# Thirty-two bytes further each time: the start addresses of the weight units and of the parts of g in a fused scan and two-layer kernel

## The chip, the core and the metric

The kernel runs on one core of one Trainium2 chip. The metric is the device time of one execution in microseconds (us). An execution was also recorded by the hardware profiler, and all rows shown here come from that one record.

## What is computed

The reference runs a gated state-space scan over 4 sequences of 768 positions with 8 heads, and sends its result through two dense layers with `h - tanh(h)` between them:

```python
# per head, in chunks along the sequence; cum = running sum of log a
M = (Cc @ Bc.T) * exp(cum_i - cum_j) * causal
y = M @ xc + (Cc @ state) * exp(cum_i)
state = exp(cum_last) * state + sum_j Bc_j x_j exp(cum_last - cum_j)
...
x = y laid out as (3072 tokens, 256)
h = x @ w_in                 # w_in  256 x 2048
g = h - tanh(h)
out = g @ w_out              # w_out 2048 x 256
```

Inputs are float32, but the two weight matrices arrive as 64-bit floats that the kernel converts on the chip.

## The kernel before

**Layers.** The tokens are cut into 12 tiles of 256 (`t`), the 2048 hidden columns into 8 units of 256 (`u`). A step is one pair (t, u). Its first part, `mm1` (line 545), makes 12 matmuls into the PSUM tile `ph`; its second, `mm2` (line 595), makes 12 into the PSUM tile `o`, where the units of a tile are summed. So there are 96 steps and 2304 matmuls of the two lines, and each is a weight load of 128 columns followed by a matmul that streams 256 columns.

**Why 12.** Each float32 operand is split into a high part, rounded to the matmul's float32r format, and the low rest: `xh`, `xl` for the input, `wh`, `wl` for the weights, `gh`, `gl` for g. A product is high by high, high by low and low by high. The stationary operand is always a 128-column piece of `wh` or `wl`; the moving operand is a 256-column piece of `xh`, `xl` (line 545) or of `gh`, `gl` (line 595).

**Around a step.** `act` takes `ph` to g: ACT's tanh (L559), DVE's subtraction (L563), ACT's rounding into `gh` (L567), DVE's rest into `gl` (L574). `g`, `gh` and `gl` each have three buffers of 128 x 512 elements in the pool `p3`. `mm2` of a step is emitted two steps after its `mm1`. Weights of a unit come once, by two DMAs, and `conv` makes `wh` (ACT, L318) and `wl` (DVE, L321) of them; both stay for the whole kernel:

```python
wh = cp.tile([P, NCONV, 2, 2, 256], F32R, name="wh")     # L284
wl = cp.tile([P, NCONV, 2, 2, 256], F32R, name="wl")     # L285
```

A unit is 2 x 2 x 256 elements, 4096 bytes in each partition.

**The scan** runs ahead of the tiles that need it, between steps. `chunk_a` makes the matmuls into `att` (lines 452 and 458: stationary operands of 9 and 16 rows), `chunk_y` those into `y` (line 494, stationary operands of 32 columns, and line 502, of 16 columns; the last chunk of a sequence has no line 502).

**Order.** The class `Order` records every operation with a cost and its dependencies, plans an order with list scheduling and random changes under a fixed seed, and emits the instructions in that order. It knows operations and named pieces of data, no addresses.

**Addresses before.** The allocator places tiles one behind another in each partition. Every unit of `wh` and `wl` starts at the same remainder after division by 512 bytes, and so do all buffers of `xh`, `xl`, `gh` and `gl`, at another; a table stands with the change.

Of the kernel before, what the change touches and what calls it, by code (L numbers as in the profile page):

```python
# [10 lines left out]
F32 = mybir.dt.float32  # L11
F32R = mybir.dt.float32r
# [4 lines left out]
ALU = mybir.AluOpType  # L17
# [3 lines left out]
P = 128  # L21
# [9 lines left out]
TT = 256  # L31
# [3 lines left out]
NCONV = NF // 2  # L35
# [6 lines left out]


NPH, NL, NSW, NRAW, NGB, LAG, WARM = 2, 3, 4, 2, 3, 2, 8
SWEEPS = 0, 2, 4, 6, 8


class Order:
# [12 lines left out]
    def slot(self, tag, bufs):  # L61
        k = self.count[tag] = self.count.get(tag, -1) + 1
        self.fresh[f"{tag}#{k}"] = tag, f"{tag}#{k - bufs}"
        return f"{tag}#{k}"
# [143 lines left out]
def tile_ssm_moe(ctx: ExitStack, tc: tile.TileContext, a, x, bn, bc, wts, out):  # L208
    nc = tc.nc
    cp = ctx.enter_context(tc.tile_pool(name="cp", bufs=1))  # L210
    p1 = ctx.enter_context(tc.tile_pool(name="p1", bufs=1))
    p2 = ctx.enter_context(tc.tile_pool(name="p2", bufs=2))
    p3 = ctx.enter_context(tc.tile_pool(name="p3", bufs=3))
# [6 lines left out]
    op = Order()  # L220
# [3 lines left out]
    raws, gs, po, n_po, obs, misc = {}, {}, {}, {}, {}, {}  # L224

    chunks, ends = {}, 0
    for t in range(NT):
        b, j = divmod(t, S // TT)
        end = b * CPB + -(-(j + 1) * TT // Q)
        chunks[t], ends = list(range(ends, end)), end  # L230
    wv, wm, pts, n_pt = {}, {}, {}, {}
    seq = {b: {} for b in range(NB)}
    KB = P * 1024

    SPAN = slice(len(chunks[0]), len(chunks[0]) + 7), slice(len(chunks[0]) + 7, NCK)


# [43 lines left out]
            op("SP", 0.42, lambda i=i: fn(i), w=[name[i]], dma=4 * KB)  # L281


    wh = cp.tile([P, NCONV, 2, 2, 256], F32R, name="wh")  # L284
    wl = cp.tile([P, NCONV, 2, 2, 256], F32R, name="wl")  # L285

    def conv(u, halves=False):
        raw, n = raws[u, 0], 2 if halves else 1
        n_v, n_m = op.pieces(slot("wv", 2), n), op.pieces(slot("wm", 1), n)

        def part(s, v):
            return v[:, s].bitcast(F32)

        def fn0(s):
            if s.start == 0:
                wv[u] = p2.tile([P, 2, 512], U32, tag="wv", name=f"wv{u}")
            nc.scalar.activation(part(s, wv[u]), raws[u][:, s, :, 1].bitcast(F32), AF.Copy, scale=REBIAS)

        def fn1(s):
            if s.start == 0:  # L300
                wm[u] = p1.tile([P, 2, 512], U32, tag="wm", name=f"wm{u}")
            nc.vector.tensor_scalar(out=wm[u][:, s], in0=raws[u][:, s, :, 0], scalar1=29, scalar2=None,
                                    op0=ALU.logical_shift_right)

        def fn2(s):
            vf = part(s, wv[u])
            nc.vector.tensor_scalar(out=vf, in0=vf, scalar1=-CLAMP, scalar2=CLAMP, op0=ALU.max, op1=ALU.min)

        def fn3(s):
            nc.vector.scalar_tensor_tensor(out=wm[u][:, s], in0=wv[u][:, s], scalar=3, in1=wm[u][:, s],  # L310
                                           op0=ALU.logical_shift_left, op1=ALU.bitwise_or)

        def fn4(s):
            nc.vector.scalar_tensor_tensor(out=wv[u][:, s], in0=wv[u][:, s], scalar=0x80000000, in1=wm[u][:, s],
                                           op0=ALU.bitwise_and, op1=ALU.bitwise_or)

        def hi(s):
            nc.scalar.copy(wh[:, u, s], part(s, wv[u]).rearrange("p i (k c) -> p i k c", k=2))  # L318

        def lo(s):  # L320
            nc.vector.tensor_tensor(out=wl[:, u, s], in0=part(s, wv[u]).rearrange("p i (k c) -> p i k c", k=2),  # L321
                                    in1=wh[:, u, s].bitcast(F32), op=ALU.subtract)

        for i in range(n):
            s, k = (slice(i, i + 1), 0.6) if halves else (slice(0, 2), 1.0)
            n_r = raw[s]
            n_h, n_l = [f"wh{u}.{j}" for j in range(2)][s], [f"wl{u}.{j}" for j in range(2)][s]
            op("ACT", 1.0 * k, lambda s=s: fn0(s), r=n_r, w=[n_v[i]])
            op("DVE", 0.8 * k, lambda s=s: fn1(s), r=n_r, w=[n_m[i]])
            op("DVE", 0.65 * k, lambda s=s: fn2(s), w=[n_v[i]])  # L330
            op("DVE", 1.35 * k, lambda s=s: fn3(s), r=[n_v[i]], w=[n_m[i]])
            op("DVE", 1.35 * k, lambda s=s: fn4(s), r=[n_m[i]], w=[n_v[i]])
            op("ACT", 1.05 * k, lambda s=s: hi(s), r=[n_v[i]], w=n_h)
            op("DVE", 1.2 * k, lambda s=s: lo(s), r=[n_v[i]] + n_h, w=n_l)
# [37 lines left out]
    def first_tile():  # L372
# [39 lines left out]
        for ck in range(len(chunks[0])):  # L412
# [12 lines left out]
            if ck in (0, 2):  # L425

                s = ck // 2
                sl = SPAN[s]
                for w in range(2):
# [9 lines left out]
    def chunk_a(ck):  # L439
# [31 lines left out]

        s = ck >= SPAN[0].stop
        op("PE", 0.65, fn_p, r=[d["n_bc"], l_c[s], r_c[s]], w=[n_a])
# [56 lines left out]
    def mm1(t, u):  # L530
        b, j = divmod(t, S // TT)
        d, ts = seq[b], slice(j * TT, (j + 1) * TT)
        cs = [c for c in range(CPB) if c * Q < ts.stop and (c + 1) * Q > ts.start]
        n_h, n_g = slot("ph", NPH), slot("g", 3)
        gs[t, u, 0] = [n_h, n_g]

        def fn():
            ph = ps_h.tile([P, 2, TT], F32, tag="ph", name=f"ph{t}_{u}")
            gs[t, u] = [ph]
            for j in range(2):  # L540

                for p in range(2):
                    for k in range(2):
                        for w_ in (wh, wl)[: 2 - p]:
                            nc.tensor.matmul(out=ph[:, j, :], lhsT=w_[:, u, 0, k, j * P : (j + 1) * P],  # L545
                                             rhs=d[("xh", "xl")[p]][:, k, ts], start=p == 0 and k == 0 and w_ is wh,
                                             stop=p == 1 and k == 1, skip_group_check=True)

        op("PE", 1.41, fn, r=[*[d["n_xh"][c] for c in cs], *[d["n_xl"][c] for c in cs], f"wh{u}.0", f"wl{u}.0"], w=[n_h])

    def act(t, u, eng):
        n_h, n_g = gs[t, u, 0]
        n_gh, n_gl = slot("gh", 3), slot("gl", 3)
        gs[t, u, 0] += [n_gh, n_gl]

        def fn_t():
            g = p3.tile([P, 2, TT], F32, tag="g", name=f"g{t}_{u}")
            gs[t, u].append(g)
            nc.scalar.activation(g, gs[t, u][0], AF.Tanh)  # L559

        def fn_s():
            ph, g = gs[t, u]
            nc.vector.tensor_tensor(out=g, in0=ph, in1=g, op=ALU.subtract)  # L563

        def fn_h():
            gh = p3.tile([P, 2, TT], F32R, tag="gh", name=f"gh{t}_{u}")
            nc.scalar.copy(gh, gs[t, u][1])  # L567
            gs[t, u].append(gh)

        def fn_l():  # L570
            _, g, gh = gs[t, u]
            gl = p3.tile([P, 2, TT], F32R, tag="gl", name=f"gl{t}_{u}")
            on = nc.vector if eng == "DVE" else nc.gpsimd
            on.tensor_tensor(out=gl, in0=g, in1=gh.bitcast(F32), op=ALU.subtract)  # L574
            gs[t, u].append(gl)

        op("ACT", 0.6, fn_t, r=[n_h], w=[n_g])
        op("DVE", 0.69, fn_s, r=[n_h], w=[n_g])
        op("ACT", 0.62, fn_h, r=[n_g], w=[n_gh])
        op(eng, 0.8 if eng == "DVE" else 1.8, fn_l, r=[n_g, n_gh], w=[n_gl])  # L580

    def mm2(t, u, seg):

        _, _, n_h, n_l = gs[t, u, 0]
        if u == seg[0]:
            n_po[t, seg] = slot("po", 1)

        def fn():
            _, _, gh, gl = gs[t, u]
            if u == seg[0]:  # L590
                po[t, seg] = ps_o.tile([P, 2, TT], F32, tag="po", name=f"o{t}_{u}")
            for k, (w_, g) in enumerate(((wh, gh), (wl, gh), (wh, gl))):
                for j in range(2):
                    for e in range(2):
                        nc.tensor.matmul(out=po[t, seg][:, e, :], lhsT=w_[:, u, 1, j, e * P : (e + 1) * P],  # L595
                                         rhs=g[:, j, :], start=u == seg[0] and k == 0 and j == 0 and e == 0,
                                         stop=u == seg[-1] and k == 2 and j == 1, skip_group_check=True)

        op("PE", 1.41, fn, r=[n_h, n_l, f"wh{u}.1", f"wl{u}.1"], w=[n_po[t, seg]])
        if u == seg[-1]:  # L600
            if u < NCONV - 1:
                keep(t, seg)
            else:
                store(t, seg)
# [102 lines left out]
    def ones(i):  # L707
        v = lt_c[:, SPAN[i]].rearrange("p c m -> p (c m)")
        nc.scalar.copy(v, nc.const_aps.tensor(1.0, (P, 1), F32).broadcast_to(v.shape))
# [85 lines left out]

    segs = [(t, tuple(range(i, j))) for i, j in zip(SWEEPS, SWEEPS[1:]) for t in range(NSW)]
    segs += [(t, tuple(range(NCONV))) for t in range(NSW, NT)]
# [15 lines left out]
    for t in range(1, NT):  # L813
        g0, n = begin["t", t - 1], begin["t", t] - begin["t", t - 1]
# [8 lines left out]
    for g in range(len(steps) + LAG):  # L823
        if g < len(steps):
            t, u, _ = steps[g]
# [54 lines left out]
```

## Time and profile before

| | |
|---|---|
| median of three executions | 346.22 us (344.73, 346.22, 346.35) |
| span of the profiled execution, first to last instruction | 344.3 us |
| instructions | 8873 |
| TensorE matmul (PE) busy | 330.2 us, 96% of the span |
| VectorE (DVE) busy | 227.5 us, 66% |
| ScalarE (ACT) busy | 192.9 us, 56% |
| GpSimd (POOL) busy | 57.2 us, 17% |

For the profiled execution the record gives the span alone, 1.9 us below the median of the three timed ones and 0.4 us below the lowest. PE is the array's matmuls, PEld its weight loads, which overlap them. A line such as `L595` is a line of the kernel. In the chain of work that ended last, a row has its start, its length and what it was; lengths there run from one start to the next, so a row of 12 matmuls divided by 12 is the distance from one matmul's start to the next one's, called the pace below.

### The profile page before, as it was taken

How to read it: one execution, taken by the hardware profiler on the slowest of the kernel's cores; microseconds unless marked ns; L12 is line 12 of the kernel's file. 1: busy time of each engine (PE TensorE's matmuls, PEld its weight loads, DVE VectorE, ACT ScalarE, POOL GpSimd, SP SyncE). 2: the span in 40 equal slices, each digit the busy share in tenths (PEclk: the TensorE clock that was granted, in tenths of full speed). 3: DMA queues.
4: the chain of work that ended last, by engine and by line, in shares of the span. 5: the costliest groups of instructions: out<-in, count | busy, mean ns of one | idle time of the engine just before them, and what ended most of it. 6: DMA issues, size and time to landing. Idle time of an engine off the chain costs nothing.

```text
span 344.3 us, 8873 instructions
## 1 busy us (share of the span) xinstructions
PE 330.2 (96%) x3756; PEld 317.9 (92%) x3756; DVE 227.5 (66%) x339; ACT 192.9 (56%) x403; POOL 57.2 (17%) x69
## 2 busy tenths in 40 slices
PE   7939979999999999999999999999999999999995
PEld 6839879999999999999999999999999999999995
DVE  5996898999998875645654655555655555654552
ACT  7855977786554543534655646444554555554441
POOL 1544453340000110101211110210401110110000
PEclk9875989999999999999999999999999999999999
DMA  7929658614000011001211200200200100000100
GB/s 164 301 63 317 179 131 201 213 52 132 3 0 3 10 51 61 32 3 45 61 45 30 63 2 9 82 2 23 71 2 1 32 2 2 32 0 2 32 0 31
DMA packets 12471, 21.39 MB, mean 62 GB/s; under 512 B 2848, under 2 KB 7648, under 8 KB 12432
## 3 DMA queue, kind: packets, MB, share of 16 engines
q1 hardware_dynamic: 12432, 20.84, 21.4%
q8 instruction: 29, 0.48, 0.6%
q14 instruction: 10, 0.08, 0.1%
HBM read 17.51 MB, written 3.32 MB: 60 GB/s over the span
## 4 chain that ended last, share of the span: by engine, by line
PE 87%; DVE 3%; SPq 3%; DMA 3%; ACT 1%; issue 1%; POOL 0%; POOLq 0%; DVEq 0%; ACTq 0%
PE o L595 40%; PE ph L545 38%; PE y L494 3%; PE att L458 2%; DMA braw<-bn_d 2%; PE cp L381 1%; DMA bc<-bc_d 1%; PE att L452 1%; SPq L770 1%; SPq L278 1%; SPq L247 1%; PE y L502 1%; PE att L392 1%; DVE wm L310 0%; SPq L772 0%
## 5 line engine op out<-in xcount | busy, mean ns | idle before, releaser
L559 ACT ACTIVATE g<-ph 128x512 f32<-128x512 f32 x96 | 57.4, 598 | 91.5 <-PE ph L545 89.3
L563 DVE TENSOR_TENSOR g<-ph,g 128x512 f32<-128x512 f32 x96 | 65.9, 690 | 62.9 <-ACT g L559 62.9
L545 PE MATMUL ph<-xh,wh 128*128 128x256 f32 x384 | 101.3, 286 | 0.0
L545 PE MATMUL ph<-xh,wl 128*128 128x256 f32 x384 | 100.0, 283 | 0.0
L574 DVE TENSOR_TENSOR gl<-g,gh 128x512 fp32r<-128x512 f32 x96 | 67.0, 700 | 26.9 <-ACT gh L567 25.7
L545 PE MATMUL ph<-xl,wh 128*128 128x256 f32 x384 | 77.1, 282 | 0.0
L567 ACT CAST gh<-g 128x512 fp32r<-128x512 f32 x96 | 59.1, 619 | 28.7 <-DVE g L563 27.2
L545 PEld LDWEIGHTS ph<-xh,wh 128*128 128x128 f32 x384 | 73.8, 192 | 1.1 <-issue 0.4
L545 PEld LDWEIGHTS ph<-xh,wl 128*128 128x128 f32 x384 | 73.8, 192 | 0.0
L469 POOL TENSOR_SCALAR_AFFINE_SELECT lt<-lt 128x896 f32<-128x896 f32 (+1 forms) x25 | 34.0, 1359 | 203.9 <-DVE lt L466 203.9
L595 PE MATMUL o<-gh,wh 128*128 128x256 f32 x384 | 63.5, 287 | 0.0
L595 PE MATMUL o<-gl,wh 128*128 128x256 f32 x384 | 60.2, 278 | 0.0
L595 PE MATMUL o<-gh,wl 128*128 128x256 f32 x384 | 60.2, 278 | 0.0
L545 PEld LDWEIGHTS ph<-xl,wh 128*128 128x128 f32 x384 | 59.8, 192 | 0.0
L595 PEld LDWEIGHTS o<-gh,wh 128*128 128x128 f32 x384 | 51.2, 188 | 2.8
L595 PEld LDWEIGHTS o<-gl,wh 128*128 128x128 f32 x384 | 51.5, 188 | 0.0
L595 PEld LDWEIGHTS o<-gh,wl 128*128 128x128 f32 x384 | 51.5, 188 | 0.0
L466 DVE TENSOR_TENSOR lt<-att,lt 128x896 f32<-128x896 f32 (+1 forms) x25 | 26.7, 1067 | 6.8 <-ACT lt L462 6.8
L462 ACT ACTIVATE lt<-att 128x896 f32<-128x896 f32 (+1 forms) x25 | 22.6, 902 | 6.1 <-PE att L458 4.4
L507 ACT COPY x<-y 16x64 f32<-16x64 f32 x96 | 19.4, 202 | 8.6 <-DVE xl L519 7.1
L494 PE MATMUL y<-lt,x 128*32 128x112 f32 (+1 forms) x448 | 17.3, 274 | 5.4 <-POOL bc L352 3.3
L494 PEld LDWEIGHTS y<-lt,x 128*32 128x32 f32 x448 | 10.2, 113 | 9.2 <-POOL bc L352 3.4
(70 smaller groups left out, 232.8 us busy)
## 6 DMA issues: line engine op xcount, KB each, us to landing
raw<-w_d SPq DMA_DIRECT2D x16, 512.0 KB
x<-x_d SPq DMA_DIRECT2D x14, 256.0 KB
bc<-bc_d SPq DMA_DIRECT2D x56, 60.0 KB
out_d<-ob SPq DMA_DIRECT2D x24, 128.0 KB
braw<-bn_d SPq DMA_DIRECT2D x14, 112.0 KB
cum<-parts SPq DMA_DIRECT2D x1, 168.0 KB
rt_c<-cum SPq DMA_DIRECT2D x4, 27.0 KB
lt_c<-cum SPq DMA_DIRECT2D x4, 27.0 KB
```

Of the source, the lines that this page charges most:

```text
L458: nc.tensor.matmul(out=at_[:, i, 2 + w, :], lhsT=bb[r, w], rhs=cc[r, w, 0:q], start=True, stop=True)
L462: nc.scalar.activation(k["l"][:, :, 0:q].rearrange("p (i w) q -> p i w q", i=4), k["a"][:, :, 0:2, :], AF.Exp)
L466: nc.vector.tensor_tensor(out=lt, in0=k["a"][:, :, 2:4, :], in1=lt, op=ALU.mult)
L469: nc.gpsimd.affine_select(out=k["l"][:, :, 0:q], in_=k["l"][:, :, 0:q], pattern=[[0, H], [1, q]], compare_op=ALU.is_ge, fill=0.0, base=N, ...
L494: nc.tensor.matmul(out=y[D * h : D * h + D, hg * Q : hg * Q + q], lhsT=d["x"][:, cg, P * hg + D * h : P * hg + D * h + D], rhs=k["l"][:, 4 ...
L507: nc.scalar.copy(grp[(ck + 1) // CPG]["x"][0:N, (ck + 1) % CPG, 2 * D * i : 2 * D * i + 2 * D], k["y"][D * i : D * i + N, H * D : H * D + ...
L545: nc.tensor.matmul(out=ph[:, j, :], lhsT=w_[:, u, 0, k, j * P : (j + 1) * P], rhs=d[("xh", "xl")[p]][:, k, ts], start=p == 0 and k == 0 an ...
L559: nc.scalar.activation(g, gs[t, u][0], AF.Tanh)
L563: nc.vector.tensor_tensor(out=g, in0=ph, in1=g, op=ALU.subtract)
L567: nc.scalar.copy(gh, gs[t, u][1])
L574: on.tensor_tensor(out=gl, in0=g, in1=gh.bitcast(F32), op=ALU.subtract)
L595: nc.tensor.matmul(out=po[t, seg][:, e, :], lhsT=w_[:, u, 1, j, e * P : (e + 1) * P], rhs=g[:, j, :], start=u == seg[0] and k == 0 and j = ...
```

## The change

Every weight unit becomes a tile of its own, and all but the last of `wh` and of `wl` are allocated 8 elements (32 bytes) longer than they are used. So are the three buffers of `gh` and the three of `gl`. The views that the instructions use have the shapes of before.

```diff
+STEP = 8
...
+    def unit(n, u):
+        v = cp.tile([P, 2 * 2 * 256 + STEP * (u < NCONV - 1)], F32R, name=f"{n}{u}")
+        return v[:, 0:1024].rearrange("p (i k c) -> p i k c", i=2, k=2)
...
-    wh = cp.tile([P, NCONV, 2, 2, 256], F32R, name="wh")
-    wl = cp.tile([P, NCONV, 2, 2, 256], F32R, name="wl")
+    wh, wl = ([unit(n, u) for u in range(NCONV)] for n in ("wh", "wl"))
...
-            nc.scalar.copy(wh[:, u, s], part(s, wv[u]).rearrange("p i (k c) -> p i k c", k=2))
+            nc.scalar.copy(wh[u][:, s], part(s, wv[u]).rearrange("p i (k c) -> p i k c", k=2))
...
-            nc.tensor.matmul(out=ph[:, j, :], lhsT=w_[:, u, 0, k, j * P : (j + 1) * P],
+            nc.tensor.matmul(out=ph[:, j, :], lhsT=w_[u][:, 0, k, j * P : (j + 1) * P],
...
+    def skewed(tag, name):
+        return p3.tile([P, 2 * TT + STEP], F32R, tag=tag, name=name)[:, 0 : 2 * TT].rearrange("p (j q) -> p j q", j=2)
...
-            gh = p3.tile([P, 2, TT], F32R, tag="gh", name=f"gh{t}_{u}")
+            gh = skewed("gh", f"gh{t}_{u}")
...
-            gl = p3.tile([P, 2, TT], F32R, tag="gl", name=f"gl{t}_{u}")
+            gl = skewed("gl", f"gl{t}_{u}")
...
-                        nc.tensor.matmul(out=po[t, seg][:, e, :], lhsT=w_[:, u, 1, j, e * P : (e + 1) * P],
+                        nc.tensor.matmul(out=po[t, seg][:, e, :], lhsT=w_[u][:, 1, j, e * P : (e + 1) * P],
```

The built program has as many instructions on every engine as before, row for row the same operations in the same order, with the same waits on the same semaphores at the same values. Only addresses differ. These are the starts within a partition, as remainders after division by 512 bytes:

| tile | before | after |
|---|---|---|
| `wh`, unit u = 0 to 7 | 128 for all | 128, 160, 192, ... 352 |
| `wl`, unit u = 0 to 7 | 128 for all | 352, 384, 416, 448, 480, 0, 32, 64 |
| `xh`, `xl` | 192 for all | 128 for all |
| `gh`, three buffers | 192 for all | 128, 160, 192 |
| `gl`, three buffers | 192 for all | 224, 256, 288 |

Inside a unit the pieces that a matmul takes begin at multiples of 512 bytes, inside `xh`, `xl`, `gh` and `gl` at multiples of 1024 bytes. All tiles that are allocated between the weights and `gh` move up by 448 bytes as a whole.

More of the change, by code (lines that the diff above doesn't have):

```diff
@@ L317, in hi @@
         def hi(s):
-            nc.scalar.copy(wh[:, u, s], part(s, wv[u]).rearrange("p i (k c) -> p i k c", k=2))
+            nc.scalar.copy(wh[u][:, s], part(s, wv[u]).rearrange("p i (k c) -> p i k c", k=2))
         def lo(s):
-            nc.vector.tensor_tensor(out=wl[:, u, s], in0=part(s, wv[u]).rearrange("p i (k c) -> p i k c", k=2),
-                                    in1=wh[:, u, s].bitcast(F32), op=ALU.subtract)
+            nc.vector.tensor_tensor(out=wl[u][:, s], in0=part(s, wv[u]).rearrange("p i (k c) -> p i k c", k=2),
+                                    in1=wh[u][:, s].bitcast(F32), op=ALU.subtract)
         for i in range(n):
```

## The prediction

> **What bounds the kernel now.** I read the page's busy shares first, then the chain of work that ended last, then that chain's rows in order of time, since the change touches nothing but where operands begin, and only a pace can show that.
>
> ```profile
> span 344.3 us, 8873 instructions
> PE 330.2 (96%) x3756; PEld 317.9 (92%) x3756; DVE 227.5 (66%) x339; ACT 192.9 (56%) x403; POOL 57.2 (17%) x69
> ...
> PEclk9875989999999999999999999999999999999999
> ...
> PE 87%; DVE 3%; SPq 3%; DMA 3%; ACT 1%; issue 1%; POOL 0%; POOLq 0%; DVEq 0%; ACTq 0%
> PE o L595 40%; PE ph L545 38%; PE y L494 3%; PE att L458 2%; DMA braw<-bn_d 2%; PE cp L381 1%; DMA bc<-bc_d 1%; PE att L452 1%; SPq L770 1%; SPq L278 1%; SPq L247 1%; PE y L502 1%; PE att L392 1%; DVE wm L310 0%; SPq L772 0%
> ```
>
> The reader is to see that 78% of the span is the chain through lines 545 and 595, that is, the 2304 matmuls, and that from the seventh slice on the array has its full clock. So the kernel's time is the number of these matmuls times their pace, plus a start of some 50 us. The pace has two values:
>
> ```profile
> 76.17 1.36 PE o L595 x12
> 77.53 1.36 PE ph L545 x12
> ...
> 115.61 2.72 PE ph L545 x24
> 118.33 0.20 PE att L452 x4
> 118.52 0.45 PE att L458 x16
> 118.97 1.61 PE o L595 x12
> 120.58 1.41 PE ph L545 x12
> ```
>
> From 76.17 to 115.61 stand 348 matmuls: 39.44 / 348 = 113.3 ns each. After the `att` matmuls the same two lines go on at 1.41 / 12 = 117.5, and over a longer piece:
>
> ```profile
> 310.41 0.47 PE y L494 x16
> 310.88 1.61 PE o L595 x12
> 312.49 1.41 PE ph L545 x12
> ...
> 332.28 1.41 PE o L595 x12
> ```
>
> 19.79 us for 168 matmuls, 117.8 ns. Where does the one pace turn into the other? Not inside a stretch, but where scan matmuls interrupt it:
>
> ```profile
> 204.94 1.41 PE ph L545 x12
> 206.35 0.52 PE y L494 x16
> 206.88 0.12 PE y L502 x16
> 206.99 1.56 PE o L595 x12
> 208.55 1.36 PE ph L545 x12
> 209.91 1.36 PE o L595 x12
> 211.27 1.36 PE ph L545 x12
> 212.63 0.21 PE att L452 x4
> 212.84 0.45 PE att L458 x16
> 213.29 1.61 PE o L595 x12
> ```
>
> After `y` with line 502 the quick pace, after `att` the slow one. In the whole trace all 20 stretches at full clock behind `att` are slow, the first at 34.7 us and the last at 304.5; so are the three behind a `y` without line 502 (the one at 310.88 is the last). Of 16 behind line 502, 11 are quick. How many matmuls run quick is read from weight loads in windows laid over the eight long quick stretches, 396 on line 595 and 420 on line 545; the first and the last window, line 595 and then line 545:
>
> ```profile
> 74.40:118.20 43.80, 23.55 (x192) 22.57 (x192) 1.00 0.11 34
> 297.50:303.80 6.30, 3.15 (x24) 2.87 (x24) 1.00 0.14 44
> ...
> 74.40:118.20 43.80, 23.70 (x192) 22.64 (x192) 1.00 0.11 34
> 297.50:303.80 6.30, 3.07 (x26) 2.87 (x24) 1.00 0.14 44
> ```
>
> With three single quick groups of 12 that makes 852. Some 60 more run at half clock early. The rest, about 1400, are slow. One pace in place of the other is worth 117.8 - 113.3 = 4.5 ns per matmul.
>
> **The change part by part.**
>
> *Order, waits, counts.* Nothing added, removed or moved on any engine or queue; cost nothing, and no cover is needed.
>
> *Writers.* `conv` writes `wh` and `wl`, `act` writes `gh` and `gl`, at other addresses.
>
> ```profile
> L574 DVE TENSOR_TENSOR gl<-g,gh 128x512 fp32r<-128x512 f32 x96 | 67.0, 700 | 26.9 <-ACT gh L567 25.7
> L595 PE MATMUL o<-gh,wh 128*128 128x256 f32 x384 | 63.5, 287 | 0.0
> L567 ACT CAST gh<-g 128x512 fp32r<-128x512 f32 x96 | 59.1, 619 | 28.7 <-DVE g L563 27.2
> L318 ACT CAST wh<-wv 128x1024 fp32r<-128x1024 f32 x7 | 7.3, 1044 | 0.9 <-DVE wv L314 0.8
> L321 DVE TENSOR_TENSOR wl<-wv,wh 128x1024 fp32r<-128x1024 f32 x7 | 8.5, 1214 | 0.0
> ```
>
> The matmuls of line 595 have no idle time ahead of them (0.0), while DVE and ACT idle 26.9 and 28.7 us ahead of `gl` and `gh`: they are early. `gh` takes 602 to 632 ns over three buffers and every neighbour that it meets:
>
> ```profile
> L567 ACT CAST gh<-g x96: 602/620/632, 30.9 to 336.6; 128x512 fp32r<-128x512 f32 x96
> ```
>
> Were each of the 192 longer by that whole spread of 30 ns, 5.8 us would be added to two engines that idle 345 - 228 = 117 and 151 us; without cover in the crowded stretch from 75 to 118 us, whose 192 matmuls of line 595 are 16 steps with 32 such writes, 1.0 us. I take 0.
>
> *Readers.* This is the only term that can matter: the pace of 2304 matmuls, whose two operands begin at a difference of 64 bytes (in remainders by 512) before, always, and at many differences after. The trace of before cannot show what another difference does, as there is no other on these lines. Its bounds: all slow ones become quick, 1400 x 4.5 = -6.3 us; all quick ones become slow, 852 x 4.5 = +3.8 us. Nearest evidence on which value to take:
>
> First, other address bits. From 76 to 115 us the matmuls run through several units, all three buffers of `gh` and `gl` and several places of `xh`, and each group of 12 takes 1.36. Whatever addresses do above 512 bytes, they do nothing.
>
> Second, other engines. In that stretch DVE was busy in 36.35 of 40 us and ACT in 21.19, writing and reading the same partitions at every phase, and the pace did not move:
>
> ```profile
> 80.00:120.00 40.00, 40.00 (x368) 39.78 (x367) 36.35 (x52) 21.19 (x34) 0.98 (x1) 1.00 0.04 14
> ```
>
> Third, the scan's own loads. The 16 matmuls of `att` at 212.84 take 0.45 us: sets of four, 112 ns per set, each with a 128-column load. They stream 112 columns and not 256, and those at 118.52, as long, stream 96:
>
> ```profile
> 118.35 0.62 PE L458 MATMUL att<-bc 16*128 16x96 f32 x16
> ```
>
> Their two operands start at differences of 0 and of 64 bytes. So 112 to 113 ns looks like what a 128-column load costs when nothing meets it, and the quick pace is the load's, with no collision left to take away. [...]
>
> [...]
>
> Fourth, the slow pace is chosen by what ran ahead, with the same addresses on both sides of the choice. That points to how loads and matmuls are staggered when a stretch starts, which the change leaves alone. I take 0, between +3.8 and -6.3, as nearest to the first, second and fourth rows.
>
> [...]
>
> *Sum.* 344.3 + 0 = 344.3 us of span for an execution like the profiled one. The median of the runs shown is 346.22, 1.9 above that span, and the runs differ by 1.6 us among themselves, as much as 360 matmuls changing pace. I forecast the next median a little below this one, 346.0, since one of three runs was at 344.73.
>
> **The rivals.**
>
> *Faster: the slow pace is a collision of the two reads at a difference of 64 bytes.* For it: the state persists for 168 matmuls, as two streams locked in step would, and a difference that changes from `wh` to `wl` and from unit to unit breaks the step. Against it: the four points above. All slow stretches quick gives 346.2 - 6.3 = 339.9; half of them 343.1.
>
> *Slower: the quick pace is the lucky stagger.* A difference that changes within every group (in line 545, `wl` begins 224 bytes further than `wh`) throws quick stretches out of step, at lines 545 and 595 between 74 and 118 us above all. At 4.5 ns it decides from about 380 of the 852 matmuls on (1.7 us); all of them give 346.2 + 3.8 = 350.0. For it: the long quick stretch hangs on one start, at 74.53. Against it: pieces there don't differ by address.
>
> [...]
>
> *The starts are drawn anew.* Behind line 502 a stretch may be quick or slow; a stretch of 48 that changes is 0.2 us, the 384 at 74.53 are 1.7. This is inside the no-change case but for that one.
>
> **How the numbers follow.** A measurement of this kernel can tell about 0.5%, 1.7 us. No change beyond that: 0.48. Faster: 0.28 for the first rival, all or part of it, and 0.03 for the third, 0.31. Slower: 0.21, the second rival with redrawn starts. The time is the likeliest's, 346.0; its own range is 344.3 to 347.7. To leave out no more than 2 in 10 the range must take in the full first rival and most of the second: 339.8 to 349.0, with 0.08 below and 0.07 above.
>
> **What would show it.** Right: rows of 1.36 and 1.41 as before, slow behind `att`, quick behind line 502, `gh` and `gl` at 619 and 700 ns. First rival: 1.36 behind `att` too. Second: 1.41 or more from 76 to 115 us, or groups within a stretch that differ by unit. [...] The forecast fails if paces take new values, or if the change of pace is no longer tied to what ran ahead.

## The result, and the profile after

The changed kernel takes 350.32 us in the median of 7 runs (348.54 to 351.27) against 346.28 for the kernel before in 7 runs beside it (344.73 to 347.42). The ratio is 1.0118, with a 95% interval from 1.0083 to 1.0153: slower by 4 us.

From the page of the changed kernel, the busy shares and the chain by line (lines 551 and 604 are what 545 and 595 were):

```profile
span 347.3 us, 8873 instructions
...
PE 332.4 (96%) x3756; PEld 319.7 (92%) x3756; DVE 227.6 (66%) x339; ACT 192.7 (55%) x403; POOL 57.3 (16%) x69
...
PE o L604 40%; PE ph L551 40%; PE y L500 3%; PE att L464 3%; DMA rt_c<-cum 2%; DMA raw<-w_d 1%; PE att L458 1%; DVE lt L410 1%; PE y L508 1%; SPq L779 1%; DMA lt_c<-cum 1%; SPq L781 1%; POOL bc L358 0%; DVE wm L308 0%; ACT x L513 0%
```

The engines are busy for nearly the same time and the chain is the same one. The long stretch that ran at 1.36 us for 12 matmuls, in the chain in order of time:

```profile
73.31 1.61 PE ph L551 x12
74.92 1.42 PE o L604 x12
76.34 1.42 PE ph L551 x12
77.75 1.40 PE o L604 x12
...
87.64 2.85 PE ph L551 x24
```

Not one group has 1.36. The groups are also no longer alike: 1.40 beside 1.42, and single distances from one matmul's start to the next one's run from 112 to 133 ns, where the kernel before had 112 to 115 in its quick stretches and 116 to 120 in its slow ones. And what ran ahead decides nothing any more:

```profile
206.43 1.43 PE ph L551 x12
207.85 0.52 PE y L500 x16
208.37 0.12 PE y L508 x16
208.49 1.62 PE o L604 x12
210.11 1.41 PE ph L551 x12
211.52 1.42 PE o L604 x12
212.94 1.40 PE ph L551 x12
214.34 0.21 PE att L458 x4
214.55 0.45 PE att L464 x16
215.00 1.62 PE o L604 x12
216.62 1.41 PE ph L551 x12
```

Behind line 508, where line 502 had given 1.36, stands 1.40 to 1.42, just as behind `att`.

Where the time came from can be closed. The same 2208 matmuls and what lies between them run from the first of these rows to the second, in the chain of before and then of after:

```profile
54.26 3.02 PE o L595 x24
340.77 0.02 issue
```

```profile
52.85 3.04 PE o L604 x24
343.72 0.02 issue
```

That is 286.51 us before and 290.87 after, 4.36 more, 1.97 ns per matmul. The start, ahead of the first row, was 1.41 us shorter in this execution of the changed kernel, with the array at half clock in other places (granted clock 0.50 from 25.8 to 34.4 us before, 0.78 from 26.0 to 34.7 us after), so the two spans differ by 3.0 only. The medians differ by 4.0.

The mean over all distances within stretches, past 51.5 us, went from 116.05 ns to 118.05. The other engines stayed where they were; the rounding into `gh`:

```profile
L576 ACT CAST gh<-g x96: 602/620/632, 31.0 to 339.6; 128x512 fp32r<-128x512 f32 x96
```

### The profile page after: what moved, and what is told of

Same layout as the page of the kernel before. It is cut to its first block, busy times and chain, and to the rows that moved or that the text cites. A ratio compares the mean times of both kernels' runs of the same rounds, so it can differ in the third digit from the quotient of the medians.

```text
span 347.3 us, 8873 instructions
## 1 busy us (share of the span) xinstructions
PE 332.4 (96%) x3756; PEld 319.7 (92%) x3756; DVE 227.6 (66%) x339; ACT 192.7 (55%) x403; POOL 57.3 (16%) x69
## 4 chain that ended last, share of the span: by engine, by line
PE 88%; DMA 4%; DVE 3%; SPq 1%; ACT 1%; issue 1%; POOL 1%
PE o L604 40%; PE ph L551 40%; PE y L500 3%; PE att L464 3%; DMA rt_c<-cum 2%; DMA raw<-w_d 1%; PE att L458 1%; DVE lt L410 1%; PE y L508 1%; SPq L779 1%; DMA lt_c<-cum 1%; SPq L781 1%; POOL bc L358 0%; DVE wm L308 0%; ACT x L513 0%
## 5 line engine op out<-in xcount | busy, mean ns | idle before, releaser
L475 POOL TENSOR_SCALAR_AFFINE_SELECT lt<-lt 128x896 f32<-128x896 f32 (+1 forms) x25 | 33.1, 1324 | 205.8 <-DVE lt L472 203.8
L604 PE MATMUL o<-gl,wh 128*128 128x256 f32 x384 | 61.0, 281 | 0.0
L604 PE MATMUL o<-gh,wl 128*128 128x256 f32 x384 | 60.9, 281 | 0.0
L604 PEld LDWEIGHTS o<-gl,wh 128*128 128x128 f32 x384 | 52.2, 188 | 0.0
L351 POOL TENSOR_TENSOR bw<-braw,wdec 128x256 f32<-128x256 f32 x14 | 13.3, 950 | 30.0 <-PE y L508 30.0
```

What stands on the lines that cost most here:

```text
L351: nc.gpsimd.tensor_tensor(out=d["b"].rearrange("p c (h n) -> p c h n", h=H), in0=d["braw"].rearrange("p c (h n) -> p c h n", h=H), in1=wd. ...
L475: nc.gpsimd.affine_select(out=k["l"][:, :, 0:q], in_=k["l"][:, :, 0:q], pattern=[[0, H], [1, q]], compare_op=ALU.is_ge, fill=0.0, base=N, ...
L604: nc.tensor.matmul(out=po[t, seg][:, e, :], lhsT=w_[u][:, 1, j, e * P : (e + 1) * P], rhs=g[:, j, :], start=u == seg[0] and k == 0 and j = ...
```

## The experiments

All kernels below have before's instructions one for one, with its waits; only addresses differ. "Difference" is the address of the first byte of the loaded weight piece less that of the streamed piece; the expectations of the moves by 32 to 128 bytes count it the other way round, so that their 96, 160 and 192 are 160, 96 and 64 modulo 256 here. A "stretch" is a run of matmuls of the two lines with no scan matmul between. "Mean pace" is the mean distance between starts within stretches past 51.5 us, without the longer gap that follows the first matmul of a stretch (220 to 228 ns in the kernel before). Each ratio is to runs of the kernel before on the same chip; the median of before differed from chip to chip, from 344.24 to 345.56 us, so that layouts are compared by ratio. The first two diffs and `STEP = 32` further down are against the changed kernel, the others against the kernel before. Several make `wh` or `wl` longer than its use, which moves whatever is allocated behind it; they share one edit, and differ in `PAD`, counted in elements of 4 bytes:

```diff
-    wh = cp.tile([P, NCONV, 2, 2, 256], F32R, name="wh")
-    wl = cp.tile([P, NCONV, 2, 2, 256], F32R, name="wl")
+    PAD = 0, 112
+
+    def weights(n, pad):
+        v = cp.tile([P, NCONV * 1024 + pad], F32R, name=n)
+        return v[:, 0 : NCONV * 1024].rearrange("p (u i k c) -> p u i k c", u=NCONV, i=2, k=2)
+
+    wh, wl = weights("wh", PAD[0]), weights("wl", PAD[1])
```

### One half of the change at a time

Units alone:

```diff
-        return p3.tile([P, 2 * TT + STEP], F32R, tag=tag, name=name)[:, 0 : 2 * TT]...
+        return p3.tile([P, 2 * TT], F32R, tag=tag, name=name)[:, 0 : 2 * TT]...
```

> Only the weight units begin 32 bytes further each; the buffers of gh and gl begin at one remainder again. Theory 'constant step' (the quick pace of 113.3 ns needs the address difference between a matmul's loaded weights and its streamed operand to stay the same from one matmul to the next): line 545 alternates between wh and wl, which now differ by 224 bytes, so no stretch keeps 113.3; mean pace 117.5 to 118.5 on both lines, time 349.5 to 351, as with the whole change. Theory 'parts of g' (the cost comes from the buffers of gh and gl): two exact paces and 346 to 347.

Measured: 350.0 us, ratio 1.0137 (1.0094 to 1.018), mean pace 118.18, distances from 112 to 133. "Parts of g" falls as the sole cause.

Parts of g alone:

```diff
-        v = cp.tile([P, 2 * 2 * 256 + STEP * (u < NCONV - 1)], F32R, name=f"{n}{u}")
+        v = cp.tile([P, 2 * 2 * 256], F32R, name=f"{n}{u}")
```

> Only the buffers of gh and gl begin 32 bytes further each; all weight units begin at one remainder, 64 bytes below xh and xl as before. Theory 'constant step': within a group of line 545 the difference is constant, but each change to line 595 and, there, from gh to gl, changes it, so the quick stretches are lost at the first change; 348 to 350.5. Theory 'weights' (only units at odd places cost): two exact paces, 346 to 347. Theory 'value' (some differences are slow and some quick, whatever ran before): line 545 keeps 113.3 in stretches, line 595 has other paces, 346.5 to 349.

Measured: 349.73 us, ratio 1.0135 (1.0092 to 1.0178), mean pace 117.76 on line 551 and 118.18 on line 604. So "weights" falls too: either half costs all of it. Two single groups of line 551 that stand between scan matmuls, and see one difference only, still ran at 113.3. The long stretch did not, although line 551 has before's difference in every matmul. That is against "value", by which line 551 would have kept 113.3 in stretches:

```profile
77.39 1.41 PE ph L551 x12
78.80 1.42 PE o L604 x12
80.22 1.41 PE ph L551 x12
```

### One difference everywhere, but another one

Everything behind the weights moved by 448 bytes, as the whole change does, with nothing moved against its neighbours (the edit above as it stands):

> No unit and no buffer is moved against its neighbours; all tiles behind the weights are moved by 448 bytes as a whole, so that weights and streamed operands begin at the same remainder (difference 0 in place of 64 bytes), everywhere the same. Theory 'constant step': again long stretches at one exact pace, none of the scatter from 112 to 133 ns; the time depends on which stretches start quick, 340 to 350. Theory 'value': one pace for all, without the choice by what ran ahead: 340 if quick, 350 or more if slow. Theory 'move as such' (the tiles behind the weights cost by being moved): 350 with the scatter.

Measured: 353.41 us, ratio 1.0236 (1.0195 to 1.0278), the slowest of the first four. The chain in order of time:

```profile
205.16 1.62 PE o L600 x12
206.78 1.44 PE ph L550 x12
208.22 1.44 PE o L600 x12
209.66 1.44 PE ph L550 x12
211.09 0.52 PE y L499 x16
211.61 0.12 PE y L507 x16
211.73 1.63 PE o L600 x12
213.36 1.44 PE ph L550 x12
```

1.44 / 12 = 120.0 ns behind `att` and behind line 507 alike: 1941 of 2145 distances are 120 ns. Hardly any scatter (116 to 121), so "move as such" falls, but a third exact pace. My "constant step", which expected long stretches at an exact pace, holds half: a constant difference gives a constant pace; "value" holds the other half, which pace it is depends on the difference.

Only `wl` moved against `wh`, by 32 bytes, and the rest kept in place modulo 512:

```diff
+    PAD = 8, 120
```

> Only wl as a whole is moved by 32 bytes against wh; all units of each and all buffers stand as before. Theory 'constant step': the one alternation inside each group of line 545 is enough to lose the quick pace there; line 545 scatters, 348 to 351. Theory 'many differences' (a loss needs units or buffers that differ among themselves): two exact paces, 345 to 347.5.

Measured: 348.31 us, ratio 1.0105 (1.0071 to 1.0139), mean pace 117.70, distances from 112 to 126. One alternation is enough, unless 224, the difference that `wl` has here, is slow by itself; no run had it alone.

### Which differences, and in what measure

Four more moves of everything behind the weights, by 32, 64, 96 and 128 bytes:

```diff
+    PAD = 0, 8
...
+    PAD = 0, 16
...
+    PAD = 0, 24
...
+    PAD = 0, 32
```

> All tiles behind the weights are moved by 32 bytes as a whole (weights 96 bytes below the streamed operands in place of 64), everywhere the same difference. Theory 'constant difference sets the pace' (what 448 bytes of the same kind showed: one exact pace of 120.0 ns): one or two exact paces with scatter of at most 3 ns, possibly others than 113.3, 117.8 and 120.0; the time is then 52 us plus 2250 times the pace, give or take 1%: 340 at 113.3 throughout, 350 at 117.8, 355 at 120. Theory 'only 0 is bad': paces and time as before, 345 to 347.

> The same with 64 bytes (difference 128). Theory 'constant difference, repeating every 128 bytes': 448 is an odd multiple of 64 as is 64, so one pace of 120.0 and 353 to 355, as with 448. Theory 'repeating every 64': already against the 448 run; would give before's two paces and 345 to 347. Theory 'each difference its own up to 512': any exact pace, 340 to 355.

> The same with 96 bytes (difference 160). Theory 'constant difference sets the pace': exact paces, time by the pace as for 32 bytes. Theory 'repeating every 64': the same paces as the 32-byte run.

> The same with 128 bytes (difference 192). Theory 'constant difference, repeating every 128 bytes': as before, 113.3 behind the y matmuls with line 502 and 117.8 behind att, 345 to 347. Theory 'each difference its own up to 512': other paces than before's, still exact.

Then two larger ones, by 256 and 384:

```diff
+    PAD = 0, 64
...
+    PAD = 0, 96
```

> All tiles behind the weights moved by 256 bytes as a whole. Theory 'modulo 128': the two paces of before and of the 128-byte run; 340 to 347. Theory 'modulo 512 or more': other exact paces, as 32, 64, 96 and 448 bytes gave (117.3 to 120.0), 347 to 354.

> All tiles behind the weights moved by 384 bytes as a whole. Theory 'modulo 128': the two paces of before, 340 to 347; which stretches are quick may differ again. Theory 'modulo 512 or more': other exact paces, 347 to 354.

Measured, sorted by the difference modulo 256:

| moved by | difference mod 256 | paces of long stretches, ns | mean pace | us | ratio (95%) |
|---|---|---|---|---|---|
| 448 | 0 | 120.0 | 119.82 | 353.41 | 1.0236 (1.0195 to 1.0278) |
| 128 | 64 | 113.3, 117.8 | 115.24 | 342.85 | 0.9931 (0.9900 to 0.9962) |
| 384 | 64 | 113.3, 117.8 | 114.50 | 341.52 | 0.9908 (0.9877 to 0.9940) |
| 96 | 96 | 117.3, 118.7 | 117.46 | 348.69 | 1.0091 (1.0053 to 1.0129) |
| 64 | 128 | 118.6, 120.0 | 118.76 | 349.73 | 1.0134 (1.0078 to 1.0190) |
| 32 | 160 | 120.0 | 119.93 | 353.6 | 1.0249 (1.0197 to 1.0302) |
| 0 (before) | 192 | 113.3, 117.8 | 116.05 | | 1 |
| 256 | 192 | 113.3, 117.8 | 116.04 | 345.15 | 0.9996 (0.9966 to 1.0027) |

A move by 256 changes nothing, not even which stretches are quick. Moves by 128 and 384 are alike in nearly every stretch (the long one from 72 us on was slow with 128 and quick with 384, which is their gap), and make most stretches behind `att` quick, which were always slow. With 384:

```profile
209.22 0.45 PE att L463 x16
209.67 1.58 PE o L600 x12
211.25 1.36 PE ph L550 x12
```

"Modulo 128" falls with 64 and 448 bytes, which have 118.6 and 120.0 in one run and 120.0 throughout in the other; "modulo 512" falls with 256. The measure is 256 bytes, shown at 64 and 192 by two places each; the other four differences have one run each, and 32 and 224 none.

A constant difference gives a stretch a constant mean, but not always a constant distance. With 160, where a scatter of at most 3 ns was expected, six distances repeat: 115, 124, 118, 121, 117 and 125 ns, 120.0 in the mean. With 128 and 96 single distances run from 112 to 124 and from 115 to 123. So scatter between single matmuls alone is no sign of a changing difference. (The times in the first of these expectations leave out the scan's matmuls: 52 us and 2250 times 113.3 ns make 307 us, not 340.)

The direct test of the 256 bytes, with buffers that differ among themselves by the whole period:

```diff
-            gh = p3.tile([P, 2, TT], F32R, tag="gh", name=f"gh{t}_{u}")
+            gh = p3.tile([P, 2 * TT + 64], F32R, tag="gh", name=f"gh{t}_{u}")[:, 0 : 2 * TT]...
```

> Only the three buffers of gh step, by 256 bytes each; weights, xh, xl, gl stay at before's places modulo 256. Theory 'only the difference modulo 256 counts' (moves of everything by 0 and 256, and by 128 and 384, gave the same paces in the same stretches): the very stretches of before at 113.3 and 117.8, ratio 0.997 to 1.003. Theory 'buffers that differ among themselves cost, whatever the step' (steps of 32 and of 128 bytes both cost 1.2 to 1.4%): scatter on line 595 and a ratio of 1.008 to 1.014.

Measured: 344.53 us, ratio 0.9982 (0.9946 to 1.0018), mean pace 116.04. Past the start the pattern of before returns, stretch by stretch:

```profile
203.06 1.41 PE ph L545 x12
204.47 0.52 PE y L494 x16
204.99 0.12 PE y L502 x16
205.11 1.56 PE o L595 x12
206.67 1.36 PE ph L545 x12
...
210.75 0.21 PE att L452 x4
210.96 0.45 PE att L458 x16
211.41 1.61 PE o L595 x12
213.01 1.41 PE ph L545 x12
```

So buffers at different places cost nothing by themselves while the difference modulo 256 stays. And the test that it is the difference, not the place of the streamed operand:

```diff
-    wh = cp.tile([P, NCONV, 2, 2, 256], F32R, name="wh")
+    wh = cp.tile([P, 16 + NCONV * 1024], F32R, name="wh")[:, 16:]
```

> The weights and everything behind them are moved together by 64 bytes: every address of a matmul's two operands is another, their difference is before's. Theory 'the difference between the two operands counts': before's two paces in before's stretches, ratio 0.996 to 1.004. Theory 'the streamed operand's own place counts': the same places of xh, xl, gh and gl as in the run that moved them alone by 64 bytes, so its paces of 118.5 and 120.0 and a ratio of 1.010 to 1.017.

Measured: 345.2 us, ratio 1.0023 (0.9995 to 1.0051), mean pace 116.04, before's stretches again. The streamed operands stand exactly where the 64-byte move alone had put them, which cost 1.3%.

### Two differences in alternation

With 64 and 192 both known as differences that have the quick pace, what does going back and forth between them cost? In the first kernel, the parts of g alone (the second diff above) in larger steps; in the second, `wl` against `wh`:

```diff
+STEP = 32
...
+    PAD = 32, 96
```

> As the run with the parts of g alone, but with steps of 128 bytes in place of 32. Theory 'only the difference modulo 128 counts': every matmul again has the difference of before in that measure, so line 545 and line 595 show 113.3 and 117.8 again and no scatter; 340 to 347, by which stretches start quick. Theory 'any change of difference from one matmul to the next costs': scatter from 112 to 127 ns and about 349.7, as with 32 bytes.

> As the run with wl moved as a whole against wh, but by 128 bytes in place of 32. Theory 'only the difference modulo 128 counts': 113.3 and 117.8 without scatter, 340 to 347. Theory 'any change of difference costs': scatter on both lines and about 348.3, as with 32 bytes.

Measured: the parts of g in steps of 128 bytes, 349.68 us, ratio 1.0118 (1.0065 to 1.0172), mean pace 117.52. `wl` moved 128 bytes against `wh`, 340.49 us, ratio 0.9874 (0.9820 to 0.9928), mean pace 114.16. Opposite results for the same two differences. Two follow-ups, the second with the `gh` edit of the 256-byte test by 32 elements beside its `PAD`:

```diff
+    PAD = 32, 64
...
+    PAD = 0, 32
+            gh = p3.tile([P, 2 * TT + 32], F32R, tag="gh", name=f"gh{t}_{u}")[:, 0 : 2 * TT]...
```

> wl is moved 128 bytes against wh, as in the run that reached 340.5, and all tiles behind by 384 in total, so that now wh stands at +64 and wl at -64 modulo 256 from the streamed operands (there it was the other way). Theory 'a difference of +64 pulls a stretch to the quick pace, -64 holds what it finds' : two thirds of the loads are now of the pulling kind; most stretches quick, 339 to 342.5. Theory 'only the order wh at -64, wl at +64 happens to fit': paces near 117.8, 346 to 350.

> All tiles behind the weights are moved by 128 bytes, and the buffers of gh step by 128 bytes more: line 545 has +64 throughout, line 595 has +64, -64, +64 by buffer for gh and -64 for gl. Theory '+64 pulls to the quick pace, -64 holds what it finds': line 545 quick, line 595 nearly so, mean pace under 115 and 339 to 343. Theory 'a step of 128 bytes among buffers costs' (as with the parts of g at 128 bytes, where line 545 had -64): mean pace 117 to 118 and 347 to 350.

Measured: the swap of signs between `wh` and `wl`, 340.5 us, ratio 0.9846 (0.9800 to 0.9893), mean pace 113.83:

```profile
204.50 0.52 PE y L499 x16
205.02 0.12 PE y L507 x16
205.14 1.57 PE o L600 x12
206.71 1.36 PE ph L550 x12
...
210.78 0.21 PE att L457 x4
210.99 0.45 PE att L463 x16
211.44 1.60 PE o L600 x12
213.04 1.36 PE ph L550 x12
214.41 1.36 PE o L600 x12
```

Quick behind `att` as well. The mixed layout: 348.38 us, ratio 1.0059 (1.0029 to 1.0090), mean pace 117.15. So "+64 pulls, -64 holds" falls, although its forecast for the swap came true. What the runs show is that alternation of 64 and 192 between `wh` and `wl` ends near the quick pace whichever sign goes where, and that with jumps by 128 among the streamed buffers the mean lies near the slow one. Why the two differ is open. The swap, and the layout it comes from, beat both kernels.

## Why the prediction was wrong

**The step that failed** is *Readers*: the term was taken as 0, between -6.3 and +3.8, and it measured +4.4 in the profile (286.51 to 290.87) and +4.0 in the medians. What the runs showed in its place is that the pace depends on the difference of the two operands' addresses modulo 256 bytes, and that streamed parts which jump by 32 or 128 bytes lose the quick pace (mean paces from 117.15 to 118.18 ns). The upper bound was wrong as well: it took the two paces of before for the only ones, while differences of 0 and 160 have 120.0 ns throughout, and a move by 32 bytes alone gives a ratio of 1.0249.

The second rival came nearest. As it said, no stretch kept the quick pace: all 852 quick matmuls were lost, and it had 350.0 where 350.32 was measured. That the number fits so well is in part luck: 852 x 4.5 ns make 3.8 us, and the profile has 4.4, because the mean is 118.05 ns and not 117.8. Another of its signs came too, groups that differ by unit: on line 551, inside stretches past 51.5 us, the groups of unit 7 take 116.9 to 117.7 ns a matmul and those of unit 5 take 118.1 to 119.4.

Its reason, that a difference which changes throws stretches out of step, is half shown. With the parts of g alone line 551 keeps before's difference, and its mean is still 117.76, where before has 116.05 over both lines. But 64 and 192 in alternation between `wh` and `wl` cost nothing. And values cost without any change: the changed kernel has all eight differences equally often, the six that were run alone have mean paces that average 117.8 to 117.9, and so prices by value would make nearly the same time. How the 4.4 us divide between values and jumps no run separates. The rival was given 0.21, and the range was cut at 349.0, a microsecond below its own time. The 0.03 for a third rival stood for a pace below 113.3, which no run shows: in its place the quickest stretches of all layouts have 113.3.

Of the four points that carried the choice:

- *First, other address bits do nothing.* True in before's trace (113.3 ns over 348 matmuls) and misused. The units and buffers of before differ by whole multiples of 512 bytes in every pair, so that these two lines had one single difference modulo 256. Indifference to multiples of 512 says nothing on 32.
- *Second, other engines don't disturb the pace.* Nothing here speaks against it: with everything moved by 448 bytes, 1941 of 2145 distances are 120 ns, whatever the other engines do. But it says nothing of the array's own two operands.
- *Third, the 112 ns of a set of four in `att` are what a load costs alone.* That was my estimate; no run shows a load alone. The figure fits the quick pace as a floor: no layout had a stretch below 113.3. But `att` was no evidence on the other differences; its own two were 0 and +64 only, with a shorter stream and sets of four. It takes 0.45 us with both, though 0 is among the slowest differences on the long lines.
- *Fourth, what ran ahead chooses the pace, so addresses don't.* This was the error of reasoning. What ran ahead chooses between two paces that one difference allows; with a difference of 0 or 160, at 120.0 ns throughout, there is nothing left to choose.

All this is at full clock. At half clock (granted clock 0.50) the matmuls of before go at 213 ns, nine from the first of these rows to the second in 1.92 us:

```profile
26.23 0.42 PE L545 MATMUL ph<-xh,wl 128*128 128x256 f32 x1
...
28.15 0.63 PE L545 MATMUL ph<-xl,wh 128*128 128x256 f32 x2
```

The changed kernel has the same distances there, seven matmuls from the first of these rows to the second in 1.50 us, 214 ns, and a difference of 160, among the slowest at full clock, has 213.4:

```profile
26.49 0.41 PE L551 MATMUL ph<-xh,wl 128*128 128x256 f32 x1
27.99 0.41 PE L551 MATMUL ph<-xh,wh 128*128 128x256 f32 x1
```

At full clock the same instructions go at 113.3 or at 120.0 by the difference of the two addresses alone.

**Right**: order, waits and writers cost 0 (`gh` 602/620/632 in both), and the 4.5 ns between the two paces of before. Of the "some 60" matmuls at half clock the trace of before has 31, which moves the lower bound by 0.1 us. The faster rival, that a difference of 64 bytes makes the slow pace, was wrong in its remedy and near in its direction: another constant difference, +64 in place of -64, gains 0.7 to 0.9%, and an alternation of the two 1.3 to 1.5%.

**Not settled**: the mechanism below the addresses, which no run shows. It would have to give the same paces at differences 256 bytes apart (shown at 64 and 192), a quick or slow pace that can last until scan matmuls interrupt it (384 matmuls at 113.3 ns, 252 at 117.8), and 213 ns at half clock whether the difference is 192 or 160. Offsets under 32 bytes were not tried, and steps of 256 between weight units were not either.

## What to carry to other kernels

When a chain of matmuls, each with its own weight load, fills the span, read the distance between starts over whole stretches: one operation with two exact paces in a single trace, as 113.3 and 117.8 ns here, is worth a test that changes nothing but addresses. Treat the layout of stationary and moving operands as one choice, try whole-block moves within a short period (here 256 bytes in steps of 32, for ratios from 0.9908 to 1.0249) before spreading buffers out, and repeat it after any change that allocates a tile ahead of them. Before using "it doesn't matter in this trace" as evidence, check that the trace has more than one value of it.

## What the runs showed of the hardware that was not expected

- For float32r matmuls of 256 streamed columns, each with a 128-column load, at full clock (granted clock 1.00), the mean pace of a stretch goes by the difference of the two operands' addresses modulo 256 bytes: 113.3 or 117.8 ns at 64 and 192, 117.3 or 118.7 at 96, 118.6 or 120.0 at 128, 120.0 at 0 and at 160.
- With a constant difference a stretch can keep one pace for hundreds of matmuls (384 at 113.3 in the kernel before and with 256 bytes). In the six layouts in which differences change by 32 bytes, or streamed buffers by 128, the mean is 117.2 to 118.2; 64 and 192 in alternation between `wh` and `wl` have 113.8 to 114.2.
- Moving tiles and nothing else moved the whole kernel from 0.985 to 1.025 of the time before (340.5 and 353.6 us, on two chips).
